# Capped attention with a gated MLP on one core: the range check's squares move, more high parts go to ScalarE, and the last output block is copied and stored in two halves

## The chip, the cores and the metric

The kernel runs on one core of one Trainium2 chip. The metric is the device time of one execution in microseconds. Five engines of the core work side by side and wait for each other by semaphores: TensorE (PE in the profile, with its weight loads as PEld), VectorE (DVE), ScalarE (ACT), GpSimd (POOL) and SyncE (SP), which here issues nearly all DMAs. Each engine takes its own instructions strictly in the order in which they were written.

## The reference, cut to what matters

```
scores = (q @ k^T) / sqrt(64)                     # 4 batches, 12 heads, 448 tokens, float32
scores = cap * tanh(scores / cap)
attn   = softmax(scores)
x      = (attn @ v), heads joined                 # 1792 tokens x 768
g, val = x @ w_gate, x @ w_val                    # 768 -> 1536
out    = (silu(g) * val) @ w_out                  # 1536 -> 768
```

The weights arrive as 64-bit floats in the device arrays and are made into 32-bit ones on the core.

## The kernel before, in words

**Stages.** The attention runs as 12 quads (two head pairs each): scores on PE (L884), tanh and exp on ACT (L888, L891), attention times values on PE (L829, L910), sums of the exponentials (L916), and on DVE the copy of each result (`xk`) and its product with the reciprocal of the sum (`x`, L847). The reciprocals go out to DRAM and come back spread over partitions (`rs` L934, `rld` L838, both on SP's queue).

**The MLP by seven products.** Both MLP layers use Strassen's scheme: a 2 x 2 block product is made of seven products of sums and differences of blocks. The up projections take 13 steps (`STEPS`, twelve chunks f of 128 hidden columns; batch pair 0 starts one step ahead of batch pair 1, so step 0 has w = 0 alone and step 12 has w = 1 alone). In a step each pair w has seven products `p` in the order of `PROD`: 1, 2, 6, 5, 7, 3, 4. The down projection (`outs(pr)`, two halves of 21 products) follows.

**High and low parts.** Every float32 operand is split into a float16 high part and a float16 low part, and a product is made of three float16 matmuls per chunk (L527 to L529 in the up projections, L702 to L704 in the down projection): high times high, low times high, high times low. The work around a product is therefore: differences of blocks (`T1` to `T4`, `oT`, DVE, L264), a high part (`XH`, `wH`, `oH`: a copy, ACT L257 or DVE L259), a low part (`XL`, `wL`, `oL`: a subtraction, DVE, L264), and behind the product the copies from PSUM (`c1`, `cu`, `c5`, ACT or DVE), the sums onto them (`c11`, `c22`, `c12`, DVE L545), silu (`gt`, ACT L560), the gate product (`va`, DVE L565) and the store of the hidden block (`hst`, SP L571). Step 1 is the first with both batch pairs; the high and low parts of pair 1 are made during it.

**The squares.** Whether float16 parts suffice is checked at run time: `square` (L315, its instruction at L322) takes the square of a block on ACT and keeps each row's sum; `fit` (L1049) reduces these sums, and a flag decides whether a slow general path runs behind everything. There are four groups: `q` (weights of the up projections, two per step for w = 0), `qx` (attention blocks, 24), `qh` (hidden blocks as they come back from DRAM for the down projection, 24 of 896 columns) and `qo` (weights of the down projection, in its first half, 21).

**What sets the order.** `Plan` (L80) is a list scheduler that runs when the kernel is built: each operation has dependencies, buffers it must get, a due time and, for each engine that may run it, a cost; `Plan.run` writes out one order for all engines. A changed cost, due time or dependency moves many instructions on ACT, DVE and SP. PE's order is pinned by dependencies from each product to the one before.

## Time and profile before

| | |
|---|---|
| median of 3 runs | 612.39 us (612.13 to 613.45) |
| the profiled execution's own time | 613.15 us |
| its span from first to last instruction | 611.1 us |
| PE busy | 592.3 us, 97% |
| DVE busy | 509.6 us, 83% |
| ACT busy | 405.1 us, 66% |
| POOL busy | 1.5 us |
| mean granted clock of TensorE | 0.997 |

Busy time counts an instruction from its modelled start to its modelled end. Matmuls overlap each other in PE's pipeline, so the busy time of PE can hide small holes between them. An engine that is not PE may be idle at no cost as long as what it makes is there before PE asks for it.

### The profile page before, as it was taken

How to read it: one execution, taken by the hardware profiler on the slowest of the kernel's cores; microseconds unless marked ns; L12 is line 12 of the kernel's file. 1: busy time of each engine (PE TensorE's matmuls, PEld its weight loads, DVE VectorE, ACT ScalarE, POOL GpSimd, SP SyncE). 2: the span in 40 equal slices, each digit the busy share in tenths (PEclk: the TensorE clock that was granted, in tenths of full speed). 3: DMA queues.
4: the chain of work that ended last, by engine and by line, in shares of the span. 5: the costliest groups of instructions: out<-in, count | busy, mean ns of one | idle time of the engine just before them, and what ended most of it. 6: DMA issues, size and time to landing. Idle time of an engine off the chain costs nothing.

```text
span 611.1 us, 9532 instructions
## 1 busy us (share of the span) xinstructions
PE 592.3 (97%) x3333; PEld 279.6 (46%) x3333; DVE 509.6 (83%) x878; ACT 405.1 (66%) x669; POOL 1.5 (0%) x11
## 2 busy tenths in 40 slices
PE   7999999999897999999999999999999899999995
PEld 2333333333353455555555555555555455555552
DVE  2779899996998999788989989897969998998830
ACT  6999999999786755545455464452768977953311
POOL 1000000000000000000000000000000000000000
PEclk9999999999999999999999999999999999999998
DMA  8586588664313355878777687767578689644111
GB/s 254 203 243 192 175 232 236 192 171 143 95 40 109 127 168 160 251 221 235 226 242 219 202 248 228 220 200 245 224 248 297 211 285 318 192 147 153 48 61 65
DMA packets 69453, 118.07 MB, mean 193 GB/s; under 512 B 13588, under 2 KB 47380, under 8 KB 69397
## 3 DMA queue, kind: packets, MB, share of 16 engines
q1 hardware_dynamic: 69362, 117.38, 61.8%
q8 instruction: 28, 0.46, 0.3%
q14 instruction: 29, 0.23, 0.1%
q0 software_dynamic: 32, 0.00, 0.0%
q10 hardware_dynamic: 2, 0.00, 0.0%
HBM read 81.79 MB, written 35.48 MB: 192 GB/s over the span
## 4 chain that ended last, share of the span: by engine, by line
PE 90%; DVE 5%; ACT 2%; DMA 1%; issue 1%; SPq 0%; ACTq 0%
PE b L527 10%; PE b L528 10%; PE b L529 10%; PE sc L884 10%; PE av L829 9%; PE b L704 7%; PE b L703 7%; PE b L702 7%; PE om L529 4%; PE om L527 4%; PE om L528 4%; PE b L916 2%; DVE B L264 2%; PE av L910 2%; DMA wf<-w 1%; PE om L704 1%
## 5 line engine op out<-in xcount | busy, mean ns | idle before, releaser
L527 PE MATMUL b<-A,w 128*128 128x448 f16 x252 | 88.8, 353 | 1.8 <-ACT c L257 1.5
L528 PE MATMUL b<-A,w 128*128 128x448 f16 x252 | 88.8, 352 | 1.1 <-DVE w L264 1.1
L529 PE MATMUL b<-A,w 128*128 128x448 f16 x252 | 88.8, 352 | 0.0
L527 PEld LDWEIGHTS <-w 128*128 128x128 f16 x504 | 49.3, 98 | 49.9 <-issue 3.4
L528 PEld LDWEIGHTS <-w 128*128 128x128 f16 x504 | 49.3, 98 | 48.8 <-issue 1.8
L529 PEld LDWEIGHTS <-w 128*128 128x128 f16 x504 | 49.3, 98 | 45.9
L257 ACT ACTIVATE c<-b 128x448 f32<-128x448 f32 x54 | 28.9, 536 | 45.1 <-PE b L704 25.3
L529 PE MATMUL om<-B,w 128*128 128x448 f16 x144 | 50.7, 352 | 0.4 <-DVE B L264 0.4
L527 PE MATMUL om<-B,w 128*128 128x448 f16 x144 | 50.8, 352 | 0.0
L528 PE MATMUL om<-B,w 128*128 128x448 f16 x144 | 50.8, 352 | 0.0
L884 PE MATMUL sc<-c,c 64*128 64x448 f32 (+1 forms) x192 | 44.9, 572 | 1.7 <-ACT w L888 1.7
L264 DVE TENSOR_TENSOR A<-A,A 128x448 f16<-128x448 f32 (+3 forms) x55 | 44.5, 828 | 1.1 <-ACT A L257 0.9
L257 ACT ACTIVATE wf<-w 128x384 f32<-128x384 f32 x37 | 20.7, 559 | 36.7 <-DMA w<-w 35.9
L888 ACT ACTIVATE w<-sc 128x896 f32<-128x896 f32 x42 | 36.9, 918 | 7.8 <-PE sc L884 7.6
L545 DVE TENSOR_TENSOR c<-c,b 128x448 f32<-128x448 f32 x60 | 37.0, 617 | 5.6 <-PE b L529 3.8
L264 DVE TENSOR_TENSOR w<-B,w 128x768 f16<-128x768 f32 x39 | 37.0, 954 | 3.4 <-ACT w L257 3.2
L704 PE MATMUL b<-B,w 128*128 128x448 f16 x108 | 38.1, 352 | 1.8 <-DVE B L264 1.8
L529 PE MATMUL b<-B,w 128*128 128x448 f16 x108 | 38.1, 352 | 1.6 <-DVE B L264 1.6
L888 ACT ACTIVATE B<-sc 128x896 f32<-128x896 f32 x42 | 36.8, 921 | 3.8 <-PE sc L884 3.6
L560 ACT ACTIVATE th<-c 128x448 f32<-128x448 f32 x48 | 26.2, 568 | 18.8 <-DVE c L565 11.4
L891 ACT ACTIVATE B<-B 128x896 f32<-128x896 f32 x42 | 38.3, 959 | 0.1
L891 ACT ACTIVATE w<-w 128x896 f32<-128x896 f32 x42 | 38.2, 956 | 0.0
(134 smaller groups left out, 1240.8 us busy)
## 6 DMA issues: line engine op xcount, KB each, us to landing
w<-w SPq DMA_DIRECT2D x72, 384.0 KB, 3.7
hidden<-c SPq DMA_DIRECT2D x48, 224.0 KB, 2.2
B<-w_S SPq DMA_DIRECT2D x24, 384.0 KB, 3.5
w<-wf SPq DMA_DIRECT2D x16, 384.0 KB, 4.5
B<-w SPq DMA_DIRECT2D x15, 384.0 KB, 5.4
th<-parts SPq DMA_DIRECT2D x48, 112.0 KB, 3.0
A<-hidden SPq DMA_DIRECT2D x12, 448.0 KB, 5.6
B<-hidden SPq DMA_DIRECT2D x12, 448.0 KB, 4.7
```

Of the source, the lines that this page charges most:

```text
L257: nc.scalar.activation(out_, in_, AF.Copy, scale=1.0 if scale is None else scale)
L264: ENG[e].tensor_tensor(out_, a, b, op=ALU.subtract)
L527: nc.tensor.matmul(o, lhsT=wh, rhs=xh, start=first, stop=False, skip_group_check=True)
L528: nc.tensor.matmul(o, lhsT=wl, rhs=xh, start=False, stop=False, skip_group_check=True)
L529: nc.tensor.matmul(o, lhsT=wh, rhs=xl, start=False, stop=end, skip_group_check=True)
L702: nc.tensor.matmul(o, lhsT=wh, rhs=xh, start=first, stop=False, skip_group_check=True)
L703: nc.tensor.matmul(o, lhsT=wl, rhs=xh, start=False, stop=False, skip_group_check=True)
L704: nc.tensor.matmul(o, lhsT=wh, rhs=xl, start=False, stop=end, skip_group_check=True)
L829: nc.tensor.matmul(T["av", u][D * i : D * i + D, :S], lhsT=T["rv", q][:, a : a + D], rhs=t_(own[j])[:, i], start=j == 0, stop=False, skip_ ...
L884: nc.tensor.matmul(z[rows, h, :S], lhsT=T["rk", w][r, keys], rhs=T["rq", w][r], start=True, stop=True)
L888: nc.scalar.activation(T["t", q, i], T["sc", q, i][:, :, :S], AF.Tanh, scale=icapr)
L891: nc.scalar.activation(T["t", q, i], T["t", q, i], AF.Exp, scale=capr)
```

## The change

Six things are altered; the matmuls and their order on PE are not.

1. `qh`: 48 squares of hidden blocks right behind `va` in the up projections, 448 columns each, in place of the 24 squares of 896 columns in the down projection. The buffer of a hidden block is held until its square is done; the differences `oT` no longer wait for a square.
2. `qx`: the 24 squares of attention blocks read the float16 high part in place of the float32 block, and are due from step 3 on, two per half chunk, in place of beside the high parts.
3. `q` is taken in steps 1 to 12 in place of 0 to 11; `qo` in the second half of the down projection in place of the first. `fit`'s due time moves with them.
4. `XH` of batch pair 0 may run on ACT too; `wH` of steps 1 and 2 and of the down projection's first half runs on ACT alone.
5. The last copy from PSUM of every output block, `ov`, and its store are split into two halves of 224 columns. For the last block of all, ACT copies and stores one half, DVE copies the other and SP stores it.
6. `LAND`, which was empty, goes; so does an engine choice in `sadd` that had one value.

```diff
-    sq = const.tile([P, 4, 24], F32, name="sq")
+    sq = const.tile([P, 4, 48], F32, name="sq")
...
-        return [], [(tag, [k for y in two for k in [("XL", *y)] + [("qx", *y)] * (y[0] in PLAIN) + [(r, y[1], y[2]) for r in READERS[y[0]]]])]
+        return [], [(tag, [k for y in two for k in [("XL", *y)] + [(r, y[1], y[2]) for r in READERS[y[0]]]])]
...
-                op(("XH", z, w, c), order, {"ACT": 0.57, "DVE": 0.39} if w else {"DVE": 0.39}, high, [raw], [(home(z, w, c), [("p", LAST[w], w, p)])])
+                op(("XH", z, w, c), order, {"ACT": 0.57, "DVE": 0.39}, high, [raw], [(home(z, w, c), [("p", LAST[w], w, p)])])
...
-                    square(("qx", z, w, c), 2, order + 3.0, 0.58, lambda z=z, c=c: T["raw", z, w, c], [raw], ("XH", z, w, c))
+                    n = 3 * PLAIN.index(z) + c
+                    square(("qx", z, w, c), 2, win_at[3] + 10.0 * n + 5.0 * w, 0.58, lambda z=z, c=c: T["xs", z, w, c][:, 0], [("p", 3 + n // 2, 1, 4)], ("XH", z, w, c))
...
-            op(key("wH", n), tw, {"ACT": 0.85 * k, "DVE": 0.56 * k}, lambda e, n=n: wH(e, n), deps, [(wtag(4 * s + n), use)])
+            op(key("wH", n), tw, {"ACT": 0.85 * k} if s in (1, 2) else {"ACT": 0.85 * k, "DVE": 0.56 * k}, lambda e, n=n: wH(e, n), deps, [(wtag(4 * s + n), use)])
...
-            op(k("c1"), at_(1), both, lambda e, g=keep: g(e, 0, "b2"), [("p", s, w, 1)], [(f"c0{cw(w)}", [("hst", 2 * w, f)])])
+            op(k("c1"), at_(1), both, lambda e, g=keep: g(e, 0, "b2"), [("p", s, w, 1)], [(f"c0{cw(w)}", [("hst", 2 * w, f), ("qh", 2 * w, f)])])
...
+                square(("qh", g, f), 3, max(end, z + 2.0) + 1.0, 0.58, lambda b=b, w=w: T["cc", s, w, b], [key("va", w, b)], ("XH", "B11", 0, 0) if s < NFC - 1 else ("oH", 0, 1, 0))
...
-                ("T2", at[1, 0] + 2.0 * c, "B22", "T1", [("oT", pr, "T1", c), ("oL", pr, 1, c), ("qh", pr, 0, 0, c)]),
+                ("T2", at[1, 0] + 2.0 * c, "B22", "T1", [("oT", pr, "T1", c), ("oL", pr, 1, c)]),
...
-            op(("wH", *key), tp - 7.0, {"ACT": 0.85, "DVE": 0.56}, wH, [("ld", *key)], [(wtag(4 * len(STEPS) + n), use)])
+            op(("wH", *key), tp - 7.0, {"ACT": 0.85} if not pr else {"ACT": 0.85, "DVE": 0.56}, wH, [("ld", *key)], [(wtag(4 * len(STEPS) + n), use)])
...
+            def ov(e, n, d=d):
+                if not n:
+                    T["ov", pr, d] = st([P, S], F32, OC[0][d])
+                z = slice(H2 * n, H2 * n + H2)
+                copy(e, T["ov", pr, d][:, z], T["ob", pr, 1, d][:, z], 2.0**-O_UP)
...
+            def ost(e, n, d=d):
+                g = batches[0] * S + H2 * n
+                (nc.scalar if e == "ACT" else nc.sync).dma_start(out[(d + NP) * P : (d + NP + 1) * P, g : g + H2], T["ov", pr, d][:, H2 * n : H2 * n + H2])
...
+            final = pr and d == last
+            op(c("ov"), end[4], {"ACT": 0.4} if final else {"ACT": 0.4, "DVE": 0.39}, lambda e, f=ov: f(e, 0), [o(4)], [(OC[0][d], [c("ost"), c("ost2")])])
+            op(c("ov2"), end[4] + 0.01, {"DVE": 0.39}, lambda e, f=ov: f(e, 1), [o(4), c("ov")] if not final else [o(4)])
+            op(c("ost"), end[4] + 0.5, {"ACT": 0.1} if final else {"SP": 0.35}, lambda e, f=ost: f(e, 0), [c("ov")])
+            op(c("ost2"), end[4] + 0.5, {"SP": 0.35}, lambda e, f=ost: f(e, 1), [c("ov2")])
...
-    fit(out_at + len(OUT_ORDER) * 3 * mm_us + 40.0)
+    fit(out_at + len(OUT_ORDER) * 6 * mm_us - 20.0)
```

What the new costs and due times do to the order is shown at three places. The first is ACT in steps 0 and 1, from the first copy behind a product (`c1` of step 0, tile c01) on. Rows with `sq` are squares; B tiles are parts of batch pair 1, w tiles parts of weights, c tiles copies from PSUM. Before:

```order
L257 ACTIVATE c01_1712<-b2_1679 128x448
L322 ACTIVATE A10_496,sq_76<-wf_1613 128x768
L257 ACTIVATE B60_1718<-B20_1102 128x448
L322 ACTIVATE B10_1416,sq_76<-B12_1095 128x448
L322 ACTIVATE B11_1525,sq_76<-B12_1095 128x448
L322 ACTIVATE B60_1718,sq_76<-B20_1102 128x448
L257 ACTIVATE c11_1750<-b2_1679 128x448
L257 ACTIVATE B62_1754<-B21_1363 128x448
L257 ACTIVATE B71_1757<-B22_1752 128x448
L257 ACTIVATE w1_1770<-wf_1613 128x384
L322 ACTIVATE B62_1754,sq_76<-B21_1363 128x448
```
The same place now:

```order
L255 ACTIVATE c01_1715<-b2_1680 128x448
L255 ACTIVATE B71_1718<-B22_1699 128x448
L255 ACTIVATE B72_1733<-B31_1483 128x448
L255 ACTIVATE c11_1747<-b2_1680 128x448
L255 ACTIVATE B41_1749<-B22_1699 128x448
L255 ACTIVATE B40_1755<-B20_1098 128x448
L255 ACTIVATE c21_1767<-b3_1736 128x448
L255 ACTIVATE w1_1771<-wf_1621 128x384
L255 ACTIVATE B70_1775<-B21_1362 128x448
L255 ACTIVATE w5_1793<-ss_1769 128x768
L255 ACTIVATE w0_1821<-ss_1773 128x768
```
The squares between the copies are gone from here, `cu` (c11) is the fourth row in place of the seventh, `c5` (c21) has come over from DVE, and the weights' high parts of step 1 (w5, w0) follow at once.

The second place is DVE in the first half of the down projection, from the sum onto output block 0 (`oc11`, L723 before and L722 now: c00, then c01, then c10) on. A and B tiles of 896 columns are differences (target equal to the first operand) and low parts; w tiles are low parts of weights. Before:

```order
L723 SCALAR_TENSOR_TENSOR c00_4719<-om_4735,c00_4719 128x448
L264 TENSOR_TENSOR A11_4312<-B62_4564,B11_4545 128x896
L264 TENSOR_TENSOR w1_4774<-B30_4686,w1_4774 128x768
L264 TENSOR_TENSOR B61_4806<-A10_4309,B71_4762 128x896
L723 SCALAR_TENSOR_TENSOR c01_4708<-om_4767,c01_4708 128x448
L264 TENSOR_TENSOR w2_4808<-B31_4698,w2_4808 128x768
L264 TENSOR_TENSOR B40_4547<-B40_4547,A40_4316 128x896
L723 SCALAR_TENSOR_TENSOR c10_4743<-om_4799,c10_4743 128x448
L264 TENSOR_TENSOR A40_4316<-B70_4567,B40_4547 128x896
L264 TENSOR_TENSOR B72_4846<-A11_4312,B41_4797 128x896
L264 TENSOR_TENSOR w3_4842<-B32_4721,w3_4842 128x768
L264 TENSOR_TENSOR B12_4861<-A40_4316,B42_4850 128x896
```
The same place now:

```order
L722 SCALAR_TENSOR_TENSOR c00_4738<-om_4765,c00_4738 128x448
L262 TENSOR_TENSOR B40_4584<-B40_4584,A40_4352 128x896
L262 TENSOR_TENSOR w1_4805<-B30_4740,w1_4805 128x768
L262 TENSOR_TENSOR A40_4352<-B70_4604,B40_4584 128x896
L722 SCALAR_TENSOR_TENSOR c01_4742<-om_4798,c01_4742 128x448
L262 TENSOR_TENSOR B72_4852<-A11_4349,B41_4795 128x896
L262 TENSOR_TENSOR w2_4841<-B31_4774,w2_4841 128x768
L262 TENSOR_TENSOR B12_4872<-A40_4352,B42_4850 128x896
L722 SCALAR_TENSOR_TENSOR c10_4772<-om_4832,c10_4772 128x448
L262 TENSOR_TENSOR w3_4876<-B32_4808,w3_4876 128x768
```
The last sum `oc11` (c10), which waits for a product, stood ahead of the last difference T2 (A40) and of the low parts B72 and B12 for the next product; now it stands behind all three.

The third place is the end of ACT's program, from the high parts of the last weights (w2, w3) on. Before:

```order
L257 ACTIVATE w2_5781<-B31_5632 128x768
L257 ACTIVATE w3_5805<-B32_5653 128x768
L257 ACTIVATE c00_5887<-b2_5349 128x448
L257 ACTIVATE c01_5908<-b1_5381 128x448
L257 ACTIVATE c10_5923<-b3_5413 128x448
```
And now:

```order
L320 ACTIVATE B61_5690,sq_76<-B32_5765 128x768
L255 ACTIVATE w2_5800<-B31_5735 128x768
L255 ACTIVATE w3_5826<-B32_5765 128x768
L255 ACTIVATE c10_5957<-b3_5422 128x224
L751 DMA out<-c10_5957 128x224
```
The copies of output blocks 0 and 1 have gone to DVE, and behind the half copy of the last block stands a DMA on ACT's own queue. DVE copies the other half, and SP stores it.

## Rows read from the trace of the kernel before

**Rows 1.** The page: the span, and engine, busy us, share, instructions.

```profile
span 611.1 us, 9532 instructions
...
PE 592.3 (97%) x3333; PEld 279.6 (46%) x3333; DVE 509.6 (83%) x878; ACT 405.1 (66%) x669; POOL 1.5 (0%) x11
```

**Rows 2.** Windows: stretch, length, busy us (instructions) of PE, PEld, DVE, ACT, POOL; clock; DMA.

```profile
145.00:168.00 23.00, 21.20 (x158) 7.30 (x148) 20.43 (x35) 19.83 (x30) 0.00 (x0) 1.00 0.41 124
168.00:192.00 24.00, 21.18 (x111) 10.63 (x110) 20.51 (x39) 19.72 (x47) 0.00 (x0) 1.00 0.22 69
192.00:216.00 24.00, 22.07 (x116) 11.04 (x115) 24.00 (x45) 16.34 (x36) 0.00 (x0) 1.00 0.37 120
216.00:456.00 240.00, 240.00 (x1271) 124.09 (x1270) 210.20 (x398) 124.33 (x239) 0.00 (x0) 1.00 0.72 220
```

**Rows 3.** Timeline of PE, where it waited: start, us, what, [idle before <-what ended it].

```profile
157.96 1.02 PE L884 MATMUL sc<-wf 64*128 64x448 f32 x4 [1.53 <-ACT B L888]
...
160.91 4.36 PE L829 MATMUL av<-B,B 128*64 128x448 f32 x22 [0.27 <-DVE B L259]
...
183.48 0.36 PE L527 MATMUL b<-A,w 128*128 128x448 f16 x1 [0.22 <-ACT w L257]
...
191.53 0.35 PE L527 MATMUL b<-A,w 128*128 128x448 f16 x1 [1.53 <-ACT c L257]
...
209.11 0.35 PE L529 MATMUL om<-B,w 128*128 128x448 f16 x1 [0.38 <-DVE B L264]
...
482.89 0.35 PE L704 MATMUL b<-B,w 128*128 128x448 f16 x1 [1.20 <-DVE B L264]
...
484.76 0.35 PE L704 MATMUL b<-B,w 128*128 128x448 f16 x1 [0.58 <-DVE B L264]
```

**Rows 4.** Windows: the whole gated MLP, from its first matmul to its last.

```profile
167.83:604.93 437.10, 430.57 (x2268) 221.55 (x2268) 374.17 (x626) 252.79 (x471) 0.00 (x0) 1.00 0.62 195
```

**Rows 5.** Windows of line L322, the squares: ACT busy us (instructions); clock; DMA.

```profile
168.00:211.00 43.00, 13.00 (x38) 1.00 0.26 80
211.00:470.00 259.00, 34.38 (x71) 1.00 0.73 227
470.00:490.00 20.00, 8.50 (x20) 1.00 0.65 205
```

**Rows 6.** Windows: from step 1's first sum on L545 to step 2's.

```profile
183.37:214.12 30.75, 26.11 (x134) 13.01 (x135) 28.78 (x51) 21.62 (x47) 0.00 (x0) 1.00 0.37 119
```

**Rows 7.** Timeline of DVE: six low parts, and a wait in the output.

```profile
196.75 3.29 DVE L264 TENSOR_TENSOR B<-B,B 128x448 f16<-128x448 f32 x6
...
480.21 0.62 DVE L723 SCALAR_TENSOR_TENSOR c<-om,c 128x448 f32<-128x448 f32 x1 [0.57 <-PE om L704]
```

**Rows 8.** Groups by line and shape: busy us, mean ns of one, idle before.

```profile
L264 DVE TENSOR_TENSOR w<-B,w 128x768 f16<-128x768 f32 x39 | 37.0, 954 | 3.4 <-ACT w L257 3.2
...
L259 DVE COPY c<-b 128x224 f32<-128x224 f32 x12 | 4.7, 388 | 0.0
```

**Rows 9.** Timeline of ACT: a wait in attention, a square, its read-out, the last copy.

```profile
156.25 0.84 ACT L257 ACTIVATE w<-ss 128x768 f16<-128x768 f32 x1 [2.71 <-DVE ss L264]
...
165.67 0.56 ACT L322 ACTIVATE A<-A 128x448 f16<-128x448 f32 x1
166.14 0.19 ACT L322 ACTIVATION_READ_ACCUMULATOR A<-A 128x1 f32 x1
...
604.97 0.54 ACT L257 ACTIVATE c<-b 128x448 f32<-128x448 f32 x1 [2.86 <-PE b L704]
```

**Rows 10.** Waits of SP: us in total, times, longest.

```profile
SPq L838 <- DVE B L847: 6.5, 1, 6.5
```

**Rows 11.** Timeline of SP: the last loads of reciprocals, and the last store.

```profile
179.91 2.58 SPq L838 DMA_DIRECT2D th<-parts  x4
...
605.53 0.33 SPq L727 DMA_DIRECT2D out<-c  x1
```

**Rows 12.** Windows: half a microsecond in the last store's flight.

```profile
606.50:607.00 0.50, 0.00 (x0) 0.00 (x0) 0.00 (x0) 0.00 (x0) 0.00 (x0) 1.00 0.94 344
```

More of the change, by code (lines that the diff above doesn't have):

```diff
@@ L203, in run @@
                 end[k] = s + d
-                end[k] += self.LAND.get(k[0], 0.0)
                 if e == "PE":
@@ L503, in step @@
         for half in range(2):
-            if 0 in ws:
-                square(key("q", half), 0, at[0] - 6.0 + 2.0 * half, 0.85, lambda half=half: gate(half).rearrange("p a b -> p (a b)"), full[half], ("XH", "B11", 0, 0))
+            if 1 in ws:
+                square(key("q", half), 0, at[0] - 6.0 + 2.0 * half, 0.85, lambda half=half: gate(half).rearrange("p a b -> p (a b)"), full[half], ("XH", "B11", s // NFC, 0))
         last = [2, 5, 3, 4]
@@ L548, in step @@
             at_ = lambda p, w=w: done[w, p]
-            op(k("c1"), at_(1), both, lambda e, g=keep: g(e, 0, "b2"), [("p", s, w, 1)], [(f"c0{cw(w)}", [("hst", 2 * w, f)])])
+            op(k("c1"), at_(1), both, lambda e, g=keep: g(e, 0, "b2"), [("p", s, w, 1)], [(f"c0{cw(w)}", [("hst", 2 * w, f), ("qh", 2 * w, f)])])
             op(k("c11"), at_(2), {"DVE": 0.62}, lambda e, g=plus: g(0, "b1"), [("p", s, w, 2), k("c1")])
-            op(k("cu"), at_(6), both, lambda e, g=keep: g(e, 1, "b2"), [("p", s, w, 6)], [(f"c1{cw(w)}", [("hst", 2 * w + 1, f)])])
+            op(k("cu"), at_(6), both, lambda e, g=keep: g(e, 1, "b2"), [("p", s, w, 6)], [(f"c1{cw(w)}", [("hst", 2 * w + 1, f), ("qh", 2 * w + 1, f)])])
             op(k("c5"), at_(5), both, lambda e, g=keep: g(e, 2, "b3"), [("p", s, w, 5)], [(f"c2{cw(w)}", [key("va", w, 1)])])
@@ L599, in hslot @@
             (0, 0): [("oT", pr, "T4", c), ("oL", pr, 6, c)], (0, 1): [("oT", pr, "T2", c), ("oL", pr, 5, c)],
-            (1, 0): [("oL", pr, 4, c)], (1, 1): [("oT", pr, "T2", c), ("oL", pr, 3, c), ("qh", pr, 1, 1, c)],
+            (1, 0): [("oL", pr, 4, c)], (1, 1): [("oT", pr, "T2", c), ("oL", pr, 3, c)],
         }[i, b]
@@ L626, in outs @@
                    [("hst", g, z), ("hst", g, z + 1)], [hslot(pr, i, b, c)])
-                square(("qh", pr, i, b, c), 3, at[1, 0] + 1.0 + 2.0 * c + (5.0 if i else 0.0), 0.92, lambda i=i, b=b, c=c: T["h", pr, c + HALF * i, b].rearrange("p a s -> p (a s)"), [("hld", pr, i, b, c)], ("oH", pr, 2, 0))
         def va(c, b):
@@ L635, in outs @@
                 ("T3", first, "B22", "B12", [va(c, 1), va(c + HALF, 1)]),
-                ("T1", first + 2.0, "B12", "B11", [("oT", pr, "T3", c), va(c, 0), ("qh", pr, 0, 1, c)]),
-                ("T2", at[1, 0] + 2.0 * c, "B22", "T1", [("oT", pr, "T1", c), ("oL", pr, 1, c), ("qh", pr, 0, 0, c)]),
-                ("T4", at[6, 0] + 2.0 * c, "B21", "T2", [("oT", pr, "T2", c), ("oL", pr, 2, c), ("qh", pr, 1, 0, c)]),
+                ("T1", first + 2.0, "B12", "B11", [("oT", pr, "T3", c), va(c, 0)]),
+                ("T2", at[1, 0] + 2.0 * c, "B22", "T1", [("oT", pr, "T1", c), ("oL", pr, 1, c)]),
+                ("T4", at[6, 0] + 2.0 * c, "B21", "T2", [("oT", pr, "T2", c), ("oL", pr, 2, c)]),
             ):
@@ L673, in outs @@
             dep = [("st", "o", a, d, j) for j in range(2)]
-            op(("ld", "o", pr, p, d), tp - 24.0, {"SP": 1.09}, load, dep, [(home_, [("wL", "o", pr, p, d)] + [("qo", p, d)] * (not pr))])
-            if not pr:
-                square(("qo", p, d), 1, tp - 6.5, 0.85, lambda p=p, d=d: T["wf", "o", 0, p, d].rearrange("p a b -> p (a b)"), [("ld", "o", 0, p, d)], ("oH", 0, p, 0))
+            op(("ld", "o", pr, p, d), tp - 24.0, {"SP": 1.09}, load, dep, [(home_, [("wL", "o", pr, p, d)] + [("qo", p, d)] * pr)])
+            if pr:
+                square(("qo", p, d), 1, tp - 6.5, 0.85, lambda p=p, d=d: T["wf", "o", 1, p, d].rearrange("p a b -> p (a b)"), [("ld", "o", 1, p, d)], ("oH", 1, p, 0))
             def wH(e, p=p, d=d, n=n):
@@ L742, in outs @@
             op(c("os12"), end[3] + 0.5, {"SP": 0.7}, lambda e, d=d: store(d, 1, T["oc", pr, 1, d]), [c("oc12")])
-            def ov(e, d=d):
-                T["ov", pr, d] = st([P, S], F32, OC[0][d])
-                copy(e, T["ov", pr, d], T["ob", pr, 1, d][:, :S], 2.0**-O_UP)
-            op(c("ov"), end[4], both, ov, [o(4)], [(OC[0][d], [c("ost")])])
-            op(c("ost"), end[4] + 0.5, {"SP": 0.7}, lambda e, d=d: store(d + NP, 0, T["ov", pr, d]), [c("ov")])
+            def ov(e, n, d=d):
[11 more added lines that the diff above has]
+            op(c("ost2"), end[4] + 0.5, {"SP": 0.35}, lambda e, f=ost: f(e, 1), [c("ov2")])
     def tile_at(q, i):
@@ L812, in sadd @@
             else:
[L813 removed]
+                nc.vector.tensor_tensor(T["tot", u], T["tot", u], t_(own[2]), op=ALU.add)
         op(("sa", u, 0), tile_at(q, own[1]) + 4.0, {"DVE": 1.14}, lambda e: sadd(e, 0), [("exp", q, own[0]), ("exp", q, own[1])], [(["B42", "B72"][upper], [("sum", q)])])
@@ L948, in gates @@
         key = lambda *a: (a[0], "w", s) + a[1:]
-        more = [key("q", half)] * (0 in STEPS[s][1])
+        more = [key("q", half)] * (1 in STEPS[s][1])
         return more + ([key("wH", 0), key("wL", 0), key("S", 2), key("S", 3), key("S", 4)] if half == 0 else [key("wL", 3), key("S", 1), key("S", 3)])
```

2 lines of the change are left out of this document (removed).

## Prediction

> **What bounds the kernel now.** I read the page first, then the waits of PE, then windows by stage. The page says that PE is busy 97% of the span [rows 1], so only time in which PE waits can be won, and what lies behind its last matmul. The windows show where PE waits: not at all between 216 and 456 us, where it starts 1271 matmuls in 240.00 us, 0.189 us apart, and for 1.80, 2.82 and 1.93 us in the three stretches from 145 to 216 [rows 2]. A matmul's modelled length is 0.35 us and its pitch 0.189, so a listed idle time of PE understates a hole by 0.16 us. The whole MLP tells the sum without that model: 2268 matmuls at 0.189 are 428.6 us, and they took 437.10 [rows 4]; 8.5 us are holes.
>
> These holes stand in two places. Six lie between 183.48 and 209.11 us (step 1), the first, the third and the last of which are shown; the two windows there list 2.82 + 1.93 = 4.75 us of idle, and six times 0.16 more make 5.7 us [rows 2, 3]. Two stand at 482.89 and 484.76, 1.78 listed, 2.1 in truth [rows 3]. The other 0.7 us are scattered. In the attention PE waits 1.53 us for a tanh and 0.27 for a copy of DVE [rows 3]. Behind the last matmul come a copy of 0.54 us, the issue of a store at 605.53, its flight, and the program's end at 611.1 [rows 1, 9, 11].
>
> **Step 1.** Here DVE is the limit: from 192 to 216 it is busy all 24.00 us [rows 2]. From the first sum of step 1 to that of step 2 DVE works 28.78 us in 51 instructions [rows 6], while PE needs 14 products of 9 matmuls, 126 x 0.189 = 23.8 us. DVE is 5.0 us over, and the holes are 5.7. In the changed order 43 instructions stand between the same two. Ten left: three low parts of 448 columns, two of weights that now come earlier, one of weights that comes later, one normalization, two copies and one high part (the last three run on ACT now), and two came (a copy and one of the weight conversion). Six low parts start within 3.29 us, so one costs 0.53 [rows 7], as do the other operations of 448 columns; a weight's low part has 0.95 us of which 0.08 overlap its neighbour, so 0.87 [rows 8]; a weight's high part I put at 0.5, between a half copy's 0.39 and that 0.95 [rows 8]. The ten are 3 x 0.53 + 3 x 0.87 + 3 x 0.53 + 0.5 = 6.3, the two 1.0. Left are 28.8 - 5.3 = 23.5 us, just under PE's 23.8.
>
> What carries the moved work? ACT spends 13.00 us of the 43 from 168 to 211 on 19 squares with their read-outs (38 instructions) [rows 5]. In the new order eight stand there: four of weights at 0.85 (the ten from 470 to 490 take 8.50 us [rows 5]) and four hidden ones at 0.56 + 0.19, less overlap 0.65 [rows 9], 6.0 us. The 7.0 us freed exceed what ACT takes over. DVE also has idle time ahead of 192: 2.57 and 3.49 us [rows 2]. And a queue is passed: SP stood 6.5 us in front of the last reciprocal loads, waiting for two normalizations on DVE [rows 10], and issued them at 179.91 [rows 11], with the weights of step 2 behind. The new order has these two normalizations among step 0's work, so that SP goes on about 4 us earlier, and the last differences, which need those loads, are no longer late.
>
> I lined up the new order of DVE and ACT against the products by hand. Everything is in time, but the low parts of T2, T1 and T3 of pair 1 come only some 0.2 us ahead of PE. So I take 0.7 us of holes as left: gain 5.0. Bounds: 5.7, and 2.5 if DVE stays some 3 us behind. It cannot fall under zero unless ACT stalls here, which is the second rival.
>
> **Output stage, first half.** DVE waits 0.57 us for a product in front of the last `oc11` at 480.21 [rows 7], and the difference and the low parts that PE wants next stand behind. The new order puts `oc11` (0.62) behind them and takes two high parts of weights and two copies (2 x 0.5 + 2 x 0.53 = 2.1) off DVE ahead of them: 0.57 + 0.53 + 2.1 = 3.2 us earlier, against a hole of 2.1. ACT's 8.50 us of squares from 470 to 490 [rows 5] go to the second half of this stage. What could be late next are the low parts behind them, with the 1.1 us that are over. Gain 1.9; bounds 0.5 and 2.1.
>
> **End of the attention.** The tanh that PE waits for stands on ACT behind a weight's high part (`wH` of step 0), which waits 2.71 us for a sum on DVE [rows 9]. Now another one stands two places earlier, waiting for a weight load, and the old one later. The load moves behind a reciprocal store on SP, about 0.5 us. PE's 1.53 us go, but then the 0.27 us place becomes the limit: the copies of the attention result on DVE come only 0.7 us earlier, since a low part has been put ahead of them. Gain 0.7; bounds 1.8 and -0.6 (a load 1.3 us later, each microsecond of which delays a tanh).
>
> **The added squares.** From step 2 on ACT gets up to 44 hidden squares and all 24 `qx`, 44 us at 0.65 each, into 240 us in which it is busy 124.33 [rows 2]. By the new order its work per step is 16.3 us at most, against PE's 23.8; DVE's is 21.0 at most, and was 210.20 / 240, about 20.8. Cover is there, so the cost is put at 0.4 for new small holes; bounds 0 and 3. If the cover fails, a late `c1`, `cu` or `c5` on ACT stops PE at once.
>
> **The tail.** A half copy on DVE takes 0.39 us in place of 0.54 on ACT [rows 8, 9]: 0.15 to 0.2. The store's data keep the 16 DMA engines 94% busy at half flight [rows 12], so one store already uses them all, and two halves move the same bytes; I give the split of the store nothing. If each half flew in half the time, 229 KB at the 344 GB/s of that row being 0.67 us, it would be 0.3 more. The Trainium skill (page Trainium Kernel Development and Optimization, section Key Constraints) says that DMAs issued from several engines share the same 16 DMA engines, and that issuing from several at once only saves the issue time. By that rule the term stays at 0.2, and without it, it would be 0.5; the 94% agrees with the rule. Gain 0.2; bounds -0.3 (a second issue, 0.33 us [rows 11]) and 0.5.
>
> `fit` comes later on DVE, but still ahead of the last three sums, behind each of which a product of 3.4 us runs on PE, so it costs nothing. `XH` on ACT in the attention replaces squares in the same places and is shorter (0.54 for a copy of this width against 0.56 + 0.19 [rows 9]).
>
> **Sum.** 5.0 + 1.9 + 0.7 + 0.2 - 0.4 = 7.4; I take 7.2, since each place has more ways to be late than early. The profiled execution took 613.15 us, 2.05 more than its span; it becomes 606.0. The median of the runs is 0.76 lower, so the forecast is 612.39 - 7.2 = 605.2 us. Within 0.2% (1.2 us, about what a measurement can tell from no change) is from 611.2 to 613.6.
>
> **Rivals.** *Step 1 stays half late.* For it: DVE's 23.5 us leave 0.3 us in a step, every wait for a product's end costs DVE itself, and PE's 0.2 us of margin are less than one instruction. Against it: the freed squares and SP's earlier loads. DVE 3 us behind there leaves 3.5 us more of holes: 605.2 + 3.5 = 608.7.
>
> *ACT becomes the one that is late.* A hidden square stands in ACT's queue right behind `va`, which is DVE's; while it waits, every copy behind it waits too. PE can bear this up to a point: from a product's end to the product that needs its copy three others run, 5.1 us, less the square (0.65) and the copy (0.45), so 4.0. If DVE brings `va` later than that by x, each of the nine steps from 2 to 10 loses x. From x = 0.9 all 7.2 + 1.2 us are gone and the kernel is slower; with x = 1, 605.2 + 9 = 614.2. For it: DVE is 88% busy in this stretch [rows 2] and waits on ACT's copies in turn. Against it: no hole at all there now, and 12% of slack that has to vanish first. With x at 0.7 to 0.9 the sum comes out as no change, 612.
>
> **Chances.** Nearly all holes go (603.2 to 607.4): 0.56. Step 1 half late (607.4 to 611.2): 0.24. More goes than I count, the attention's 1.8 first (under 603.2): 0.04. No change: 0.09. Slower: 0.07. So faster 0.84, same 0.09, slower 0.07. The range from 602.8 to 610.6 leaves out the no-change and slower cases and little else.
>
> **What would show it.** In the changed profile PE should have at most a microsecond of holes between 183 and 210 us, none near 480, and 2268 matmuls in about 429.5 us. ACT should show squares on c tiles all through the up projections, busy some 150 of 240 us, with short waits for DVE's `va`. DVE should stay near 24 of 24 us in step 1 and yet be in time. The last copies should be 224 columns wide on both engines. Holes of PE ended by ACT's copies between 216 and 456 us would make the second rival true; holes ended by DVE's low parts in step 1 the first.

## The result, and the profile after

The changed kernel takes **606.49 us** (median of 5 runs, 605.44 to 608.91), before 612.39 in runs beside it: a ratio of 0.991, 95% interval 0.9884 to 0.9936. The forecast was 605.2, faster. A second measurement on another chip gave 606.41 against 614.61, 0.9866 (0.9844 to 0.9889).

The page of the profiled execution (606.26 us), to be read beside [rows 1]:

```profile
span 604.5 us, 9598 instructions
...
PE 590.3 (98%) x3333; PEld 279.6 (46%) x3333; DVE 509.4 (84%) x880; ACT 416.0 (69%) x721; POOL 1.6 (0%) x11
```

The windows of [rows 2], the whole MLP [rows 4], and DVE from step 1's first sum to step 2's [rows 6]; columns as there:

```profile
145.00:168.00 23.00, 21.77 (x156) 7.94 (x153) 21.16 (x36) 19.85 (x28) 0.00 (x0) 1.00 0.43 130
168.00:192.00 24.00, 24.00 (x129) 12.43 (x127) 21.49 (x39) 16.64 (x33) 0.00 (x0) 1.00 0.28 75
192.00:216.00 24.00, 24.00 (x129) 12.40 (x128) 22.98 (x43) 17.53 (x39) 0.00 (x0) 1.00 0.48 152
216.00:456.00 240.00, 239.21 (x1266) 123.62 (x1265) 211.50 (x400) 147.91 (x340) 0.00 (x0) 1.00 0.72 224
...
166.54:596.70 430.16, 429.37 (x2272) 221.83 (x2268) 371.70 (x626) 264.73 (x535) 0.00 (x0) 1.00 0.62 198
...
182.15:206.72 24.57, 24.57 (x132) 12.70 (x131) 23.49 (x43) 20.26 (x46) 0.00 (x0) 1.00 0.39 123
```

Step 1 has no listed idle of PE left (24.00 of 24.00, twice). DVE does there what was counted: 43 instructions, 23.49 us. The MLP went from 437.10 to 430.16 us (the window of [rows 4] begins 0.07 us behind its first matmul, which starts at 167.76). ACT, which has all the hidden squares now, is busy 147.91 of 240 us. All waits of PE from the end of the attention on are these (timeline of PE, compare [rows 3]):

```profile
158.11 0.59 PE L892 MATMUL sc<-c,c 64*64 64x448 f32 x2 [0.63 <-ACT B L896]
...
159.70 4.73 PE L837 MATMUL av<-B,B 128*64 128x448 f32 x24 [0.60 <-DVE B L257]
...
421.18 0.35 PE L526 MATMUL b<-A,w 128*128 128x448 f16 x1 [0.79 <-ACT c L255]
```

The two near 480 are gone, and one is new: at 421 PE waits for a copy of ACT. What ACT did ahead of that copy (timeline of ACT: a wait for weights, two of the three squares behind it, and the copy):

```profile
417.11 0.55 ACT L255 ACTIVATE wf<-w 128x384 f32<-128x384 f32 x1 [1.57 <-DMA w<-w]
...
419.33 0.58 ACT L320 ACTIVATE A<-c 128x448 f16<-128x448 f32 x1 [0.20 <-DVE c L564]
...
420.03 0.58 ACT L320 ACTIVATE A<-c 128x448 f16<-128x448 f32 x1
...
420.61 0.53 ACT L255 ACTIVATE c<-b 128x448 f32<-128x448 f32 x1
```

SP issues the last loads of reciprocals at 173.50, in place of 179.91 [rows 11], and so the loads behind them (timeline of SP):

```profile
173.50 2.58 SPq L846 DMA_DIRECT2D th<-parts  x4
```

The program's end, as a timeline of all engines (PE's last rows left out; compare [rows 9, 11]), and the DMA behind it in half microseconds (the last two numbers are the share of the 16 DMA engines and GB/s):

```profile
596.74 0.36 ACT L255 ACTIVATE c<-b 128x224 f32<-128x224 f32 x1 [19.59 <-PE b L703]
597.12 0.38 ACTq L751 DMA_DIRECT2D out<-c  x1
597.13 0.39 DVE L259 TENSOR_SCALAR c<-b 128x224 f32<-128x224 f32 x1 [3.11 <-ACT c L255]
597.54 0.33 SPq L751 DMA_DIRECT2D out<-c  x1
```
```profile
598.50:599.00 0.50, 0.00 (x0) 0.00 (x0) 0.00 (x0) 0.00 (x0) 0.00 (x0) 1.00 0.65 200
599.00:599.50 0.50, 0.00 (x0) 0.00 (x0) 0.00 (x0) 0.00 (x0) 0.00 (x0) 0.55 0.07 16
...
600.00:600.50 0.50, 0.00 (x0) 0.00 (x0) 0.00 (x0) 0.00 (x0) 0.00 (x0) 0.50 0.06 18
600.50:601.00 0.50, 0.00 (x0) 0.00 (x0) 0.00 (x0) 0.00 (x0) 0.00 (x0) 0.50 0.01 2
```

DVE's half copy starts when ACT's has ended, not beside it. Most data are through by 599.0, and a share of 0.06, which is what one of 16 engines makes, goes on to 600.6. From the start of the last copy to the end of the span it is 7.76 us, before 6.13 (604.97 to 611.1).

**Where the 6.6 us of the two spans lie.** Up to the start of the fourth group of scores 0.61 (10.80 to 10.19); from there to the MLP's first matmul 0.61; the MLP 7.0 (start of its first matmul to start of its last: 167.76 to 604.58, and 166.54 to 596.35); behind it -1.63. The first is chance: over all 14 profiles of this study that group starts between 9.72 and 11.12, in the changed kernel's second profile at 10.69.

### The profile page after: what moved, and what is told of

The parts are those of the page before. It is cut to its first block, busy times and chain, and to the rows that moved or that the text cites. A ratio compares the mean times of both kernels' runs of the same rounds, so it can differ in the third digit from the quotient of the medians.

```text
span 604.5 us, 9598 instructions
## 1 busy us (share of the span) xinstructions
PE 590.3 (98%) x3333; PEld 279.6 (46%) x3333; DVE 509.4 (84%) x880; ACT 416.0 (69%) x721; POOL 1.6 (0%) x11
## 4 chain that ended last, share of the span: by engine, by line
PE 90%; DMA 3%; DVE 3%; ACT 2%; issue 1%; SPq 0%; ACTq 0%; DVEq 0%
PE sc L892 10%; PE b L526 10%; PE b L527 10%; PE b L528 10%; PE av L837 9%; PE b L703 7%; PE b L702 7%; PE b L701 7%; PE om L527 4%; PE om L526 4%; PE om L528 4%; DMA w<-w 3%; PE b L924 2%; PE av L918 2%; PE om L703 1%; PE om L702 1%
## 5 line engine op out<-in xcount | busy, mean ns | idle before, releaser
L255 ACT ACTIVATE c<-b 128x448 f32<-128x448 f32 (+1 forms) x51 | 27.0, 532 | 47.8 <-PE b L703 28.0
L255 ACT ACTIVATE w<-B 128x768 f16<-128x768 f32 x31 | 26.1, 841 | 20.3 <-PE b L703 16.0
L527 PE MATMUL b<-B,w 128*128 128x448 f16 x108 | 38.1, 352 | 0.0
L526 PE MATMUL b<-B,w 128*128 128x448 f16 x108 | 38.1, 352 | 0.0
L702 PE MATMUL b<-B,w 128*128 128x448 f16 x108 | 38.1, 352 | 0.0
```

The lines of the kernel that those rows point to most:

```text
L255: nc.scalar.activation(out_, in_, AF.Copy, scale=1.0 if scale is None else scale)
L526: nc.tensor.matmul(o, lhsT=wh, rhs=xh, start=first, stop=False, skip_group_check=True)
L527: nc.tensor.matmul(o, lhsT=wl, rhs=xh, start=False, stop=False, skip_group_check=True)
L702: nc.tensor.matmul(o, lhsT=wl, rhs=xh, start=False, stop=False, skip_group_check=True)
```

## Experiments

Each was run beside the kernel before on the same chip; its median was 612.7 to 614.6 there, so ratios are compared, and holes of PE by profile.

### The tail

Run t1 copies and stores the last block whole:

```diff
+            if final:
...
+                op(c("ov"), end[4], {"ACT": 0.54}, whole, [o(4)], [(OC[0][d], [c("ost")])])
+                op(c("ost"), end[4] + 0.5, {"SP": 0.7}, lambda e, d=d: store(d + NP, 0, T["ov", pr, d]), [c("ov")])
+                continue
```

> The changed kernel, but its very last output block is copied whole by ACT (448 columns) and stored whole by SP, as in the kernel before. Everything else stands as changed. In the changed kernel's profile 8.0 us lie between the start of the last matmul (596.51) and the end (604.5); before the change they were 6.5 (604.58 to 611.1). Theory A, the split of copy and store is what made the tail longer: the tail goes back to 6.5 us and the time falls by 1.5, to about 605.0. Theory B, the tail is longer for a reason that has nothing to do with the split (what the DMA engines do besides at the end, or chance of one execution): tail and time stay, 606.5 within 0.5. My forecast of the split (gain 0.2) would make this kernel 0.2 slower, 606.7.

Measured: 605.21 us, ratio 0.9849 (0.9821 to 0.9877). From the copy's start (596.77) to the end (603.4) 6.63 us. The store and its data:

```profile
597.34 0.33 SPq L726 DMA_DIRECT2D out<-c  x1
```
```profile
599.50:600.00 0.50, 0.00 (x0) 0.00 (x0) 0.00 (x0) 0.00 (x0) 0.00 (x0) 1.00 0.00 0
...
600.50:601.00 0.50, 0.00 (x0) 0.00 (x0) 0.00 (x0) 0.00 (x0) 0.00 (x0) 1.00 0.13 34
601.00:601.50 0.50, 0.00 (x0) 0.00 (x0) 0.00 (x0) 0.00 (x0) 0.00 (x0) 1.00 0.07 20
```

So the tail is short again, as theory A has it. The data do not end earlier for that: after a pause the last eight packets of the store move from 600.17 to 601.12 by the trace's DMA records, 0.5 us later than the changed kernel's last data (600.57). Run t2 gives the halves a tile each:

```diff
...
+                    T["ov", pr, d, n] = st([P, 6 * P], F32, "ss")[:, z] if n else st([P, S], F32, OC[0][d])[:, z]
...
```

> The changed kernel, but the two halves of the last block are copied into two separate tiles, so that DVE's half copy need not wait for ACT's (in the changed kernel's profile it starts at 597.13, right after ACT's end at 597.10). Still ACT stores one half and SP the other. Theory A1, the copies one after the other are what the split lost: DVE's copy starts 0.4 us earlier, the tail is 7.6 us or less and the time 606.1. Theory A2, the second queue is what is late (its packets come on a queue of their own): the tail stays at 7.6 to 8.0 and the time at 606.1 to 606.5, the landing of the stores not earlier by more than 0.4.

Measured: 605.97 us, 0.9864 (0.9837 to 0.9891); copy to end 7.66 us. DVE still starts behind ACT (596.73, ACT's copy from 596.34): with the output tiles apart, what the halves still share is the PSUM tile that both read. So this run says nothing on copies side by side. The Trainium skill (PSUM — Partial Sum Buffer, section PSUM bank collisions raise a hardware error) says that two engines cannot access one bank within the same partition at the same time; the 0.03 us between the end of ACT's half and the start of DVE's agree with a program that keeps them apart. Run t3 lets SP issue both stores:

```diff
-            op(c("ost"), end[4] + 0.5, {"ACT": 0.1} if final else {"SP": 0.35}, lambda e, f=ost: f(e, 0), [c("ov")])
+            op(c("ost"), end[4] + 0.5, {"SP": 0.35}, lambda e, f=ost: f(e, 0), [c("ov")])
```

> As the run with two tiles, but SP issues both stores, one after the other on its own queue; ACT issues none. Theory A2, ACT's queue is what is late: the tail falls to 6.4 to 6.9 us (the second issue is 0.33 later than the first), the time to about 605.2. Theory A1 or B: the tail stays at 7.6 to 8.0, the time at 606.1 to 606.5.

Measured: 606.23 us, 0.9869 (0.9842 to 0.9896); copy to end 7.92 us, though ACT issues nothing:

```profile
597.38 0.33 SPq L755 DMA_DIRECT2D out<-ss  x1
597.81 0.65 SPq L755 DMA_DIRECT2D out<-c  x1
```

So the split costs the time, whichever queue carries it. Five profiles with it have 7.66 to 7.92 us from copy to end, the two of the changed order with a whole block 6.63 and 6.78: 1.1 us.

**Where this time is lost.** Behind its last issue SP reads the flag, branches on it past the general path, waits for eight semaphores, among them those of the last stores, and the program closes. These instructions of SP in the kernel before, in the changed one and in t1 (by line: how many, their length in ns, the start of the first and the last):

```profile
L1125 SPq EVENT_SEMAPHORE  x8: 17/17/17, 609.0 to 609.6; - x8
...
L1125 SPq COMPARE_BRANCH  x1: 50/50/50, 606.5 to 606.5; - x1
```
```profile
L1133 SPq EVENT_SEMAPHORE  x8: 17/17/17, 601.7 to 602.3; - x8
...
L1133 SPq COMPARE_BRANCH  x1: 50/50/50, 598.5 to 598.5; - x1
```
```profile
L1141 SPq EVENT_SEMAPHORE  x8: 17/17/17, 600.9 to 601.9; - x8
...
L1141 SPq COMPARE_BRANCH  x1: 50/50/50, 598.3 to 598.3; - x1
```

From the start of the copy to the branch it is 1.5, 1.8 and 1.5 us, from the branch to SP's next instruction 2.5, 3.2 and 2.6, and from there to the end 2.1, 2.8 and 2.5. The copies in series are the 0.2 ahead of the branch (copy to last issue 0.80 in place of 0.57). The next 0.7 come behind the branch: in the five profiles with halves SP goes on 3.0 to 3.4 us after it, in the nine with a whole block 2.5 to 2.8. SP does not wait for the last data there: its first wait is for an older store, and in t1 it passes it at 600.9, ahead of the last data. The last half store of the changed kernel is issued at 597.54 and lands 3.5 us later, at 601.1 (the last number of its DMA row), also before SP goes on at 601.7:

```profile
out<-c SPq DMA_DIRECT2D x1, 112.0 KB, 3.5
```

In all five profiles with halves SP goes on 0.6 to 0.7 us behind this landing; the two may have a cause in common, which no run shows. Most of the last 0.7 is a pause of 0.5 to 0.6 us ahead of SP's last DRAIN, in the four profiles in which ACT and SP store a half each. In t1 the eight waits take 1.0 us in place of 0.6: there, and in v1 below, the late data do hold SP, for 0.5 us, so that a whole block too has a longer tail in the changed order (6.63 and 6.78) than in the old one (6.02 to 6.57 in seven profiles).

Why the data end late is in the DMA records too. In t1 a packet of 16 KB of an instruction queue moves from 598.39 to 600.18, and the last eight packets of the store begin at 600.17 and follow one another; in the changed kernel that packet moves from 597.85 to 599.62. In ten of the 14 profiles 8 to 16 packets of the last store begin only as this packet ends, and the data end 3.1 to 4.5 us behind the copy's start; in the other four none stands behind it, and they end 2.3 to 2.6 us behind. That one DMA engine carries both is inferred from these times. Late data alone need not cost anything: in b1 and b2 below they end 0.5 us later than in the kernel before (3.1 us behind the copy in place of 2.6), and the tail is as long (6.0 and 6.1 us).

### The hole at 421

Run s1 moves squares behind copies on ACT, five in all:

```diff
+    for f in range(1, NFC):
+        for g in (3, 2):
+            x = (("qh", g, f - 1), "ACT")
...
+            if to > n:
+                at = order.index(act[to])
+                order.remove(x)
+                order.insert(at, x)
```

> The changed kernel, but five of the hidden squares on ACT (four kept places in steps 2, 3, 10 and 11) stand behind the copies c1 and cu of the next step instead of ahead of them; no other engine's order changes. In the changed kernel's profile PE has one hole in the MLP, at 421.18 (0.79 us listed, ended by ACT's copy c1, in front of which ACT works through three squares, 418.47 to 420.6). Theory C, the squares make this hole: it goes, PE waits nowhere between 166.5 and 596.5, and the time falls by 0.9 to about 605.6; if such holes also make the spread of the runs (605.4 to 608.9), the spread narrows to about 1 us. Theory D, the late loads of weights ahead of it make the hole (SP and DVE are late there, and ACT waits): a hole of the same size stays at the same place, ended by something else, and the time stays at 606.5.

Measured: 608.70 us, 0.9908 (0.9881 to 0.9934), 2.7 us above t2 on the same chip. The hole at 421 is gone, and a larger one is there (PE, and the first load of hidden blocks on SP, at 421.31 in t2):

```profile
432.77 0.35 PE L526 MATMUL om<-B,w 128*128 128x448 f16 x1 [2.61 <-ACT c L255]
```
```profile
423.51 1.27 SPq L614 DMA_DIRECT2D A<-hidden  x3
```

A square writes its unneeded result into a corner of tile A10, and this load fills A10: it waits for the squares (waits of SP from 415 to 430 us: total, times, longest):

```profile
SPq L614 <- ACT A L320: 2.8, 1, 2.8
```

Run v1 has the squares of step 11 write into a tile of pair 1, and the last block whole:

```diff
...
-                square(("qh", g, f), 3, max(end, z + 2.0) + 1.0, 0.58, lambda b=b, w=w: T["cc", s, w, b], [key("va", w, b)], ("XH", "B11", 0, 0) if s < NFC - 1 else ("oH", 0, 1, 0))
+                square(("qh", g, f), 3, max(end, z + 2.0) + 1.0, 0.58, lambda b=b, w=w: T["cc", s, w, b], [key("va", w, b)], ("XH", "B11", 1 if s == NFC - 2 else 0, 0) if s < NFC - 1 else ("oH", 0, 1, 0))
...
```

> A version meant to beat both: the changed kernel with the last block copied whole by ACT and stored whole by SP, with the five hidden squares behind the copies c1 and cu, and with the unused result of step 11's squares written into a tile of batch pair 1 instead of the one that the first hidden load of the down projection goes into. In the run with the squares moved alone that load was issued at 423.51 in place of 421.31, behind the squares at 422.12 and 422.82, its data held a high part on ACT, and a hole of 2.61 us opened at 432.77. If the shared tile made that hole, PE has no hole between 166 and 596 now, and the time is 0.9 under the run with the whole last block alone. If the late squares themselves made it, a hole of 1 us or more stays near 432.

Measured: 604.16 us (603.21 to 604.68), 0.983 (0.9808 to 0.9852). The load is back at 421.30; 1.8 us of the hole are gone, not all:

```profile
430.78 0.35 PE L526 MATMUL om<-B,w 128*128 128x448 f16 x1 [0.79 <-ACT c L255]
```
```profile
427.76 0.95 ACT L255 ACTIVATE A<-A 128x896 f16<-128x896 f32 x1 [1.47 <-DMA A<-hidden]
```

ACT now waits for the hidden blocks ahead of the next copy: the 0.8 us have moved by 10 us, not gone, and the MLP is as long as in the changed kernel (429.80 and 429.81 us from first to last start). Neither theory's forecast came: the shared tile made 1.8 us of the hole, and the next limit, the hidden loads, leaves 0.8. Moving the squares does not shorten the MLP. By the row at 417.11 ACT's wait of 1.57 us for weights has a part in the hole at 421 too; no run took that wait away. The changed kernel beside it:

> The changed kernel itself once more, beside the mended version on the same chip, to see what of its profile is chance: the 8.0 us from the last matmul's start to the end, the hole of 0.79 us at 421, and the start of the attention (the fourth group of scores at 10.19, against 10.80 before). If these are the kernel's own, they come back: 7.7 to 8.3 us, 0.7 to 1.0 us, and a start between 9.7 and 10.9 that varies from run to run without a link to the kernel.

Measured: 606.41 us. Copy to end 7.86, the hole 0.77 at 421.98, the MLP 429.78: its own, not chance. From the last matmul's start it is 8.2 us, and 8.1 in the first profile, whose last matmul starts at 596.35, not at the 596.51 expected. v1 is 2.25 us faster than it in the medians. Its profiled span is 2.5 shorter: 1.1 by the whole last block, the rest ahead of the MLP, 0.97 of that in the start that varies.

### What closed the holes of step 1 and near 480

These runs start from the kernel before. Listed idle of PE from 183 to 209 us, and at 480 to 485:

| run | step 1 | near 480 | ratio to before (95%) |
|---|---|---|---|
| before | 4.75 | 1.78 | 1 |
| b1, 63 squares gone | 4.06 | 1.78 | 0.9992 (0.9977 to 1.0008) |
| b2, six operations to ACT | 4.10 | 1.78 | 1.001 (0.9987 to 1.0033) |
| b3, loads early on SP | 3.22 | 1.78 | 0.9975 (0.9959 to 0.9991) |
| b4, all three | 2.08 | 1.78 | 0.9952 (0.993 to 0.9975) |
| b5, and ten squares and ten operations more | 2.07 | 1.78 | 0.994 (0.9918 to 0.9962) |
| b6, b4 and two sums moved | 1.61 | see below | 0.9943 (0.9929 to 0.9956) |
| after | 0 | 0 | 0.991 (0.9884 to 0.9936) |

```diff
...
+    gone = {k for n, k in enumerate(seen) if k[0] in ("q", "qx") and lo - 8 < n < hi} | {k for k in seen if k[0] in ("qh", "qo")}
+    order = [x for x in order if x[0] not in gone]
```

> The kernel before, without the 18 squares that ACT takes between step 0's first copy and step 2's first sum, and without the 45 squares of the down projection (left out: the range check reads a constant in their place). No other instruction moves; DVE, PE and SP keep their order. It asks how much of the gain comes from the squares leaving ACT alone. Before, the holes of PE are 5.7 us in step 1 (183 to 209 us, 4.75 listed) and 2.1 near 482 to 485 (1.78 listed). Theory S, ACT's squares make the step 1 holes (they delay high parts, copies and silus, and through these DVE): listed idle in step 1 falls under 1.5 us, time about 4 us less. Theory D, DVE's 28.8 us of work against PE's 23.8 make them: DVE's work is the same, so 3.5 to 4.8 us of listed idle stay. For the output stage, my forecast's step (the place of oc11 and four more operations on DVE) leaves the holes at 482 to 485 as they are; if ACT's squares there make them, they go (2.1 us).

```diff
+    moved = {("c5", 0, 0), ("c1", 1, 1), ("cu", 1, 1), ("wH", "w", 2, 1), ("cu", 2, 0), ("cu", 2, 1)}
+    order = [(k, "ACT" if k in moved else e) for k, e in order]
```

> The kernel before, with six operations of steps 0 to 2 put from DVE to ACT, in their places of the order, as the changed kernel has them: the copies c5 of step 0, c1 and cu of step 1's pair 1, cu of step 2 (both pairs), and one high part of weights (wH of step 2). The squares stay. In step 1 DVE does 2.1 us less (3 operations), ACT 2.0 more. Theory D, DVE's work makes the holes of step 1: listed idle falls by about 2 us, from 4.75 to 2.7. Theory S, ACT is the one that is late: ACT gets later still, the holes stay at 4.75 or grow.

```diff
...
+    early = [order[seen.index(("ld", "w", 2, n))] for n in range(2)]
...
+    n = [k for k, _ in order].index(("rld", 20))
+    order[n:n] = early
```

> The kernel before, with only SP's order changed: the two loads of step 2's weights stand ahead of the last reciprocals' four loads, in front of which SP stands 6.5 us. In the kernel before these loads are issued at 182.53, ACT waits 1.96 us for the first one (high part at 186.67), the silu behind it comes late, and DVE waits 1.76 us for that silu (190.26). Theory P, this late load is a large part of the holes (ACT's wait, then DVE's): the weights come before 180, ACT's and DVE's waits go, and the listed idle of step 1 falls by 1.5 to 2, from 4.75 to about 3. Theory D or S, DVE or ACT would be late without it too: the waits move elsewhere, listed idle stays within 0.5 of 4.75.

Neither the squares nor DVE's work alone is worth more than 0.7 us. Without the squares the holes that ACT ended go, but two that DVE's low parts end grow (1.07 to 1.47, 1.37 to 2.03); and b2 has a new one of 0.52 us at 437, ended by DVE. The loads are worth 1.5: in b3 they go out at 171.59, and of the six holes exactly the one that ACT's copy ended (1.53 at 191.53 [rows 3]) is gone, the other five as long as before. PE's rows of b3:

```profile
182.12 0.36 PE L527 MATMUL b<-A,w 128*128 128x448 f16 x1 [0.22 <-ACT w L257]
...
183.55 0.36 PE L528 MATMUL b<-A,w 128*128 128x448 f16 x1 [1.07 <-DVE w L264]
...
194.36 0.35 PE L529 MATMUL b<-B,w 128*128 128x448 f16 x1 [1.37 <-DVE B L264]
...
198.11 0.35 PE L529 MATMUL b<-B,w 128*128 128x448 f16 x1 [0.18 <-DVE B L264]
```

Run b4 has the three edits together:

> The kernel before with all three edits: without those 63 squares (left out: the range check reads a constant for them), with the six operations on ACT, and with the early loads on SP. The order of low parts, differences and normalizations on DVE is still that of before. If these three carry the gain, listed idle of PE in step 1 falls from 4.75 to under 0.7 and near 480 to 0 or 1.8 as in the run without squares; time about 7 us under before. If the order of the low parts on DVE carries it (three low parts and two of weights that come earlier in the changed kernel, two normalizations ahead of differences), 1.5 to 3 us stay.

Its holes:

```profile
184.58 0.36 PE L528 MATMUL b<-A,w 128*128 128x448 f16 x1 [1.47 <-DVE w L264]
...
194.46 0.35 PE L529 MATMUL b<-B,w 128*128 128x448 f16 x1 [0.43 <-DVE B L264]
...
479.38 0.35 PE L704 MATMUL b<-B,w 128*128 128x448 f16 x1 [1.20 <-DVE B L264]
...
481.25 0.35 PE L704 MATMUL b<-B,w 128*128 128x448 f16 x1 [0.58 <-DVE B L264]
```

```diff
...
+    moved |= {("XH", "T2", 0, 0), ("XH", "T2", 0, 1), ("XH", "T2", 0, 2), ("XH", "T1", 0, 1), ("XH", "B22", 0, 2), ("wH", "w", 0, 3)}
+    moved |= {("wH", "o", 0, 2, 0), ("wH", "o", 0, 2, 2), ("oc1", 0, 0), ("oc1", 0, 2)}
```

> The kernel before with all engine moves and with the squares gone, but in the order of before: as the run with all three edits, and also the ten squares of the late attention and step 0 left out (the range check reads a constant), six operations of the late attention put from DVE to ACT (five high parts of batch pair 0 and one half high part of weights), and in the down projection two high parts of weights and the first copies of two blocks put from DVE to ACT; there no sum, difference or low part changes its place. The run with all three edits left 2.1 us of listed idle in step 1 (1.47 of it before a weight's low part at 184.58) and 1.78 near 480. If the work that DVE was freed of is what counts, step 1 falls under 0.5 (DVE comes to that low part some 2.4 us earlier), and the 1.78 of the output stage fall under 0.3 (2.1 us of work gone ahead of those low parts). If the new order of low parts and sums counts, 1 to 2 us stay in step 1, and 1 or more in the output stage. If ACT is late with what it was given, PE's holes are ended by ACT. Time 8 us under before in the first case, 5 in the second.

More freed work changes nothing there: 2.07 and 2.08, and near 480 the same 1.20 and 0.58, to the hundredth, in the kernel before and in b1 to b5. (b5 has a new hole of 1.20 us at 396, ended by a sum of DVE, so its time says less than its holes.) A wait that no freed work shortens may be set by an order. In each place a sum that waits for PE stands on DVE ahead of what PE wants next (DVE's timeline in b4):

```profile
183.03 0.62 DVE L545 TENSOR_TENSOR c<-c,b 128x448 f32<-128x448 f32 x1 [0.54 <-PE b L529]
...
476.70 0.62 DVE L723 SCALAR_TENSOR_TENSOR c<-om,c 128x448 f32<-128x448 f32 x1 [0.52 <-PE om L704]
```

So b6 moves two sums:

```diff
...
+    behind(("c11", 1, 0), ("wL", "w", 1, 2))
+    behind(("oc11", 0, 2), ("oL", 0, 6, 2))
```

> The run with all three edits (the kernel before without 63 squares, for which the range check reads a constant, six operations on ACT, early loads), and in it just two instructions of DVE in another place: the first sum of step 1 (c11, at 183.03 there, in front of which DVE waits 0.54 us for a product) stands behind the low parts of step 1's weights instead of ahead of them, and the last oc11 of the first output blocks (476.70 there, 0.52 us of waiting) stands behind the last difference T2 and two low parts. No work is added, taken away or given to another engine. The holes 1.47 at 184.58 and 1.20 + 0.58 at 479.38 and 481.25 have been 1.1 to 1.5, 1.20 and 0.58 in every kernel so far with these sums in front, whatever DVE or ACT had been freed of. Theory O, a sum that waits for PE stands in front of the low part that PE wants next: listed idle in step 1 falls from 2.08 to 0.5 to 1.0, near 480 from 1.78 to 0 to 0.3, time 2.5 us below the run with all three edits. Theory D, DVE has too much work there: a sum of 0.53 us that moves by three places changes nothing in the amount, PE waits for the next low part or for the sum, and 1.5 or more stay in each place.

In this run the store of that output block keeps its place and goes out ahead of the moved sum, so that 128 x 448 outputs lack one product; the sum also waits for the store, which the theory has no part in. PE's rows, and the moved sum on DVE:

```profile
184.11 0.36 PE L528 MATMUL b<-A,w 128*128 128x448 f16 x1 [0.47 <-DVE w L264]
...
194.51 0.35 PE L529 MATMUL b<-B,w 128*128 128x448 f16 x1 [0.96 <-DVE B L264]
...
478.41 0.35 PE L704 MATMUL b<-B,w 128*128 128x448 f16 x1 [0.18 <-DVE B L264]
...
480.28 0.35 PE L704 MATMUL b<-B,w 128*128 128x448 f16 x1 [0.57 <-DVE B L264]
...
482.24 0.35 PE L704 MATMUL b<-A,w 128*128 128x448 f16 x1 [0.66 <-DVE A L264]
```
```profile
480.56 0.62 DVE L723 SCALAR_TENSOR_TENSOR c<-om,c 128x448 f32<-128x448 f32 x1 [0.34 <-DMA out<-c]
```

The first hole of each place shrinks by about what stood ahead, 1.47 to 0.47 and 1.20 to 0.18: the order made that much of them. In step 1 half comes back 10 us later (0.43 to 0.96), in front of another low part of DVE; that DVE has too much to do there is likely, but no run shows it. So neither theory's forecast came whole: 1.61 are left in step 1, and the median is not told apart from b4's (0.9943 and 0.9952). Near 480 the later two waits (0.57 and 0.66) are not readable, because of the store. In the changed kernel the sum runs without a wait, behind the low parts (DVE's timeline):

```profile
473.16 1.08 DVE L262 TENSOR_TENSOR B<-A,B 128x896 f16<-128x896 f32 x1
474.17 0.62 DVE L722 SCALAR_TENSOR_TENSOR c<-om,c 128x448 f32<-128x448 f32 x1
```

## Why the prediction was right, and where not

**Step 1** (5.0 forecast, bounds 2.5 to 5.7): 5.7, all of it. DVE's new amount was right to the instruction, but the reason was too simple. Of 4.75 listed us the three edits take 2.67, of which SP's early loads alone 1.53. The prediction had seen these loads, but put no price of their own on them. SP went on 6.4 us earlier (179.91 to 173.50), not about 4. The moved sum takes 0.47 more; the 1.61 left fall, by elimination, to the rest of DVE's new order (low parts and normalizations earlier), which wasn't taken apart.

**Output stage** (1.9; 0.5 to 2.1): 2.1. The step "0.57 + 0.53 + 2.1" is wrong in its largest number: the four operations that left DVE and ACT's squares moved PE by 0.00. The sum's place takes 1.02 of the 1.78 listed, as b6's first hole shows, close to its 0.57 and 0.53; that it also closes the rest is argued from the changed kernel's order alone.

**End of the attention** (0.7): 0.6. As forecast the tanh's 1.53 became 0.63, and DVE's copy limits next, 0.60 in place of 0.27. The size may have some luck in it: the two waits together are 1.34 to 1.80 in the seven profiles of the old order (1.80 in the one beside) and 1.01 to 1.30 in the seven of the new.

**Added squares** (-0.4; 0 to -3): -0.95 (0.79 listed and 0.16), at one place, the same in both profiles of the changed kernel. It is the second rival's mechanism, ACT's copies late behind hidden squares, in one step and not in nine, and behind a wait for weights that the rival did not have.

**The tail** is the term that was mis-sized: +0.2 (bounds -0.3 to 0.5), measured -1.63 between the two profiles, of which the split makes 1.1. The step that failed is "a half copy on DVE takes 0.39 us in place of 0.54": the halves run one after the other, and the last issue comes 0.23 us later in place of 0.15 to 0.2 earlier. And the sum had nothing for what stands behind the last store: from SP's branch on the flag to the end it is 4.6 us before and 6.0 after, 0.7 of it between the branch and SP's next instruction and 0.7 behind that. The bound of 0.3 for a second issue on SP was too small as well. That a second queue brings no faster flight holds: the Trainium skill (Trainium Kernel Development and Optimization, section Key Constraints) says that all queues share the 16 DMA engines and that a second one saves only issue time, and t3 agrees, whose tail is 0.26 us longer than t2's with a second issue 0.42 us later.

Together 5.7 + 2.1 + 0.6 - 0.95 - 1.63 = 5.8, and the start's 0.6 makes 6.4 of the 6.6 profiled; the scattered holes are the rest. In the medians the gain is 5.9 and the forecast 7.2; the tail, 1.8 under its forecast, is more than the miss, and step 1 gave some back. The first rival (step 1 half late) did not come.

**Open:** why SP goes on 0.7 us later behind its branch with two halves. In the changed kernel DVE, ACT and SP branch within 0.8 us of each other (597.8, 597.9 and 598.5) and go on 3.2 to 3.7 us later; in the kernel before they branch at 595.4, 605.3 and 606.5 and go on 2.5 to 2.9 us later. No run moved a branch alone, so this stays a guess. Open too is the pause ahead of SP's last DRAIN.
